# Windowed attention in four query groups of 144, its score and value products in eight array tiles, PSUM with fixed places

## The chip, the cores and the metric

One NeuronCore of a Trainium2 chip runs the whole program; the other cores are idle. The metric is the device time of one execution in microseconds. The engines are TensorE (PE, with its weight loads shown apart as PEld), VectorE (DVE), ScalarE (ACT), GpSimd (POOL) and SyncE (SP), which issues the DMAs. Each engine works through its own instructions in order.

## The reference

Eight batches of eight heads attend over 576 positions with a head dimension of 64. The first four heads see the last 32 positions, the last four see every fourth of the last 128, so that both kinds look at 32 keys. The result is a matrix of 4608 tokens by 512, which goes through a dense layer, a softmax gate with a normalisation, and a second dense layer.

```python
scores = scale * np.matmul(q, k.transpose(0, 1, 3, 2))
mask_plain = (rel >= 0) & (rel < window)                      # window = 32
mask_dil = (rel >= 0) & (rel < window * dilation) & (rel % dilation == 0)   # dilation = 4
attn = softmax(where(mask, scores, -1e9)); attn_out = attn @ v
x = attn_out.transpose(0, 2, 1, 3).reshape(B * S, H * D)      # 4608 x 512
h = x @ w_in                                                  # 512 -> 1024
solu = h * softmax(h)
ln = (solu - mean) / sqrt(var + 1e-06) * g_ln
out = ln @ w_out                                              # 1024 -> 512
```

## The kernel before

**Units.** A unit is one batch and one pair of heads; there are 32, numbered by batch and, inside a batch, by pair. Pairs 0 and 1 are plain heads, pairs 2 and 3 dilated ones, whose positions the host has sorted into four classes of 144, so that the same 32-wide window serves both. Queries go in blocks of 32, each against 64 keys (its own block and the one before).

**A unit's front** (`scores`, `soft_max`, `soft_exp`, `soft_inv`, `soft_norm`). `scores` multiplies in two parts, s0 and s1, into two PSUM tiles `ps_s0` and `ps_s1`. The 576 queries are split into two halves of nine blocks; the two heads lie on partitions 0 to 63 and 64 to 127 of `kt`, and the stationary operand `qt` has zeros where the other head is, so that one matmul over 128 rows and 64 columns gives both heads of a block (L163). VectorE adds the mask into `sm` (L171), takes the maximum (L187), GpSimd subtracts it (L188), ScalarE takes the exponential (L202), VectorE sums, inverts and multiplies (L204 to L214). For units 2, 3 and 4 the mask goes in by a matmul with an identity instead, and the exponential reads PSUM.

**A unit's back** (`probs_t`, `attend`, `spread`). VectorE transposes the probabilities in 32x32 blocks to `pt` (L221). `attend` multiplies them with `vt` in array tiles of 32 rows by 64 columns, four of the eight tiles in use, into `ps_x` and `ps_t1` (L235). `spread` copies the result, half by half, to the dense layer's operand: ScalarE writes the rounded part `x_hi` (L257) and VectorE the rest, `x_lo` (L258).

**A tile's dense part.** Each of 36 tiles of 128 tokens goes through `moe_h` (two halves of 12 matmuls into `ps_h`, L277), `moe_act` (VectorE's negated maximum `nmax` L288, ScalarE's exponential `e` L291), `moe_gate` (VectorE's product `t` L298, mean `mu` L306 and centring L307), `moe_var` (ScalarE and GpSimd), `moe_t` (eight transposes on TensorE into `ps_t0` and `ps_t1`, L336, copied out as `th` and `tl`) and `moe_o` (24 matmuls into `ps_o`, L351, of the tile before).

**Order.** The weights are converted and units 0 to 4 run in hand-written ticks, in which the order of all engines is that of the text. From the first tile on only TensorE's order is written (five lists `LEADS`, then `STEP` for every further tile); a scheduler orders the other engines. In `STEP`, on TensorE, a tile's dense layer h0 to h3 comes first, then x0 (`attend` of the unit whose front was in the step before), then s0 and s1 (`scores` of the next unit), then o (`moe_o`), then t (`moe_t`). 22 of the steps have both an x0 and the scores after it, four have x0 alone, three have scores alone, the last five neither.

**PSUM.** Eight pieces of one bank each, or two: `ps_s0`, `ps_s1`, `ps_x`, `ps_t0`, `ps_t1`, `ps_o` and `ps_h` (two). The scores share no piece with another step; `ps_t1` serves both `attend` and `moe_t`.

Of the kernel before, what the change touches and what calls it, by code (L numbers as in the profile page):

```python
# [68 lines left out]
def windowed_attention_then_solu_kernel(  # L69
# [70 lines left out]
    def scores(n, part):  # L140

        qt, kt = loaded[n]["q"], loaded[n]["k"]
        dil = int(n % NPAIR >= NPAIR // 2)
        if part == 0:
            st[n] = {"sm": att.tile([P, NU, WQ], F32, name="sm")}
        sm = st[n]["sm"]
        us = range(0, 5) if part == 0 else range(5, NU)
        nu = len(us)
# [1 line left out]
        ps = ps_a.tile([P, 512], F32, name=f"ps_s{part}")  # L150
        ps = ps[:, 0 : 5 * WQ].rearrange("p (u w) -> p u w", w=WQ)
        st[n]["ps", part] = ps
        mk = mask_sb[:, dil, us[0] : us[0] + nu, :]
# [6 lines left out]
        for i, u in enumerate(us):  # L160
            for par in range(2):
                qb = NU * par + u
                nc.tensor.matmul(  # L163
                    out=ps[64 * par : 64 * par + 64, i, :],
                    lhsT=qt[:, qb, :],
                    rhs=kt[:, WIN * qb : WIN * qb + WQ],
                    start=not on_pe,
                    stop=not on_pe or i == nu - 1,
                )
# [4 lines left out]

    def soft_max(n):
        sm = st[n]["sm"]
        mx = small.tile([P, NU], F32, name="mx")
        if n in PE_MASK:
            st[n]["mx"] = mx
            for part, (u0, u1) in enumerate(((0, 5), (5, 9))):  # L180
                nc.vector.tensor_reduce(
                    out=mx[:, u0:u1], in_=st[n]["ps", part][:, 0 : u1 - u0, :],
                    axis=AX.X, op=ALU.max, negate=True,
                )
# [2 lines left out]
        nc.vector.tensor_reduce(out=mx, in_=sm, axis=AX.X, op=ALU.max)  # L187
        nc.gpsimd.tensor_tensor(  # L188
            out=sm, in0=sm, in1=mx.unsqueeze(2).broadcast_to([P, NU, WQ]), op=ALU.subtract
        )  # L190

    def soft_exp(n):
        sm = st[n]["sm"]
        if n in PE_MASK:
            rs = st[n]["rs"] = small.tile([P, NU], F32, name="rs")
            for u in range(9):
                nc.scalar.activation(
                    out=sm[:, u, :], in_=st[n]["ps", u // 5][:, u % 5, :], func=AF.Exp,
                    bias=st[n]["mx"][:, u : u + 1], scale=0.125, accum_out=rs[:, u : u + 1],
                )  # L200
            return
        nc.scalar.activation(out=sm, in_=sm, func=AF.Exp, scale=0.125)  # L202
# [14 lines left out]

    def probs_t(n):

        pt = st[n]["pt"] = att.tile([P, NU * WQ], F32, name="pt")  # L220
        nc.vector.transpose(out=pt, in_=st[n]["sm"].rearrange("p u w -> p (u w)"))  # L221

    def attend(n):

        vt = loaded[n]["v"]
        pt = st[n]["pt"]
        b, pr = divmod(n, NPAIR)
        out = [ps_a.tile([P, 512], F32, name="ps_x"), ps_m.tile([P, 512], F32, name="ps_t1")]
        for i in range(NV):
            u0, u1 = max(i - 1, 0), min(i + 1, NU)  # L230
            k0, k1 = max(WQ * i - WIN, 0), min(WQ * i + WIN, NU * WQ)
            for par in range(2):
                for h in range(2):
# [1 line left out]
                    nc.tensor.matmul(  # L235
                        out=out[par][64 * h : 64 * h + 64, WIN * u0 : WIN * u1],
                        lhsT=vt[r : r + WIN, i, :],
                        rhs=pt[r : r + WIN, k0:k1],
                        start=i == 0,
                        stop=i == NV - 1,  # L240
                        skip_group_check=True,
                    )
        for half in range(2):
            spread(n, out[half][:, 0:HALF], half)

    def spread(n, ps, half):
        b, pr = divmod(n, NPAIR)
        base = (b % 2) * S

        def view(x):  # L250
            x = x[:, pr, base : base + S]
            if pr < NPAIR // 2:
                return x[:, half * HALF : half * HALF + HALF]
            return x.rearrange("p (i c) -> p c i", c=DIL)[:, 2 * half : 2 * half + 2, :]

        src = ps if pr < NPAIR // 2 else ps.rearrange("p (c i) -> p c i", c=2)
        nc.scalar.copy(out=view(x_hi), in_=src)  # L257
        nc.vector.tensor_tensor(  # L258
            out=view(x_lo), in0=src, in1=view(x_hi).bitcast(F32), op=ALU.subtract
        )  # L260
# [24 lines left out]
    def moe_act(i):  # L285
        h = ms[i]["h"].rearrange("p a b -> p (a b)")
        nmax = small.tile([P, 1], F32, name="nmax")
        nc.vector.tensor_reduce(out=nmax, in_=h, axis=AX.X, op=ALU.max, negate=True)  # L288
# [2 lines left out]
        nc.scalar.activation(out=e, in_=h, func=AF.Exp, bias=nmax, scale=1.0, accum_out=se)  # L291
# [256 lines left out]
def _mask():  # L548
    m = np.full((P, 2, NU, WQ), NEG, np.float32)
    c = np.arange(WQ)  # L550
    for u in range(NU):
        for p in range(P):
            qb = NU * (p // 64) + u
            q = WIN * qb + p % WIN
            k = WIN * (qb - 1) + c
            ok = (k >= 0) & (q - k >= 0) & (q - k < WIN)
            m[p, 0, u, ok] = 0.0
            m[p, 1, u, ok & (k // CLS == q // CLS)] = 0.0
    return m
# [47 lines left out]
```

## Time and profile before

| | |
|---|---|
| median of three runs | 577.02 us (576.15 to 577.3) |
| the profiled execution | 577.16 us, of which the span from the first to the last instruction is 575.1 us |
| TensorE's granted clock, mean | 0.967 |
| DMA, mean over the span | 102 GB/s |

How to read it: the profile gives one execution. Busy shares are of the span; the chain that ended last tells which work the end hung on, and a timeline gives the start and the length of single instructions in microseconds. Ends of matmuls are modelled, so the distance between the starts of two matmuls says more than their length. A matmul on float32 operands shows as two instructions.

### The profile page before, as it was taken

To read this page: it belongs to the slowest core of one execution; us is meant where nothing else is said; L and a number is where in the kernel's file an instruction comes from. 1 tells how busy PE (TensorE), PEld (TensorE's weight loads), DVE (VectorE), ACT (ScalarE), POOL (GpSimd) and SP (SyncE) were. 2 spreads that over 40 slices of the span, in tenths; PEclk is the share of its full clock that TensorE was granted. 3 is DMA by queue.
4 is the path that set the end of the run, shared out by engine and by line. 5 is a ranking of instruction groups with operands and counts; after the bars stand their busy time and mean duration, and the time that the engine had idled before them with its cause. 6 is when DMAs were issued, how large, how long until landed. Compare 5 with 4: busy or idle time off the path is not lost.

```text
span 575.1 us, 13371 instructions
## 1 busy us (share of the span) xinstructions
PE 531.8 (92%) x5740; PEld 442.2 (77%) x5740; DVE 356.7 (62%) x617; ACT 225.5 (39%) x451; POOL 153.9 (27%) x280
## 2 busy tenths in 40 slices
PE   3464859999999999999999999999999999999996
PEld 2353648888888888888888888888888888888885
DVE  4988995645666666655666666646666666634342
ACT  3467753343333333333333333333333333333232
POOL 2654771212222222211222222211222222211111
PEclk9966779999999999999999999999999999999999
DMA  8786620312333333323232333222333310001000
GB/s 316 233 305 248 200 73 34 106 61 88 103 106 104 105 104 99 103 58 98 96 110 95 106 105 106 98 83 81 114 105 103 96 49 19 19 19 38 18 19 36
DMA packets 22090, 58.40 MB, mean 102 GB/s; under 512 B 2704, under 2 KB 3088, under 8 KB 22032
## 3 DMA queue, kind: packets, MB, share of 16 engines
q1 hardware_dynamic: 22032, 57.55, 30.1%
q8 instruction: 45, 0.74, 0.5%
q14 instruction: 13, 0.11, 0.0%
HBM read 48.11 MB, written 9.44 MB: 100 GB/s over the span
## 4 chain that ended last, share of the span: by engine, by line
PE 83%; DVE 8%; ACT 3%; issue 2%; DMA 2%; POOL 1%; SPq 0%; ACTq 0%; DVEq 0%
PE ps_h L277 34%; PE ps_o L351 32%; PE ps_x L235 5%; PE ps_s L163 5%; PE ps_t L336 5%; DVE mag L399 1%; PE ps_t L235 1%; DVE nmax L288 1%; DVE mag L414 1%; DMA raw<-w_out 1%; DMA mask_sb<-mask 1%; ACT e L291 1%; POOL sm L188 1%; DVE rs L204 1%; DVE mag L407 1%
## 5 line engine op out<-in xcount | busy, mean ns | idle before, releaser
L277 PE MATMUL ps_h<-wi_hi,x_hi 128*128 128x512 f32 x288 | 117.6, 408 | 7.5 <-ACT x_hi L257 5.3
L351 PE MATMUL ps_o<-wo_hi,th 128*128 128x512 f32 x288 | 116.2, 404 | 0.8 <-ACT th L338 0.8
L277 PE MATMUL ps_h<-wi_hi,x_lo 128*128 128x512 f32 x288 | 114.2, 397 | 0.0
L277 PE MATMUL ps_h<-wi_lo,x_hi 128*128 128x512 f32 x288 | 113.7, 395 | 0.0
L351 PE MATMUL ps_o<-wo_hi,tl 128*128 128x512 f32 x288 | 113.1, 393 | 0.0
L351 PE MATMUL ps_o<-wo_lo,th 128*128 128x512 f32 x288 | 113.1, 393 | 0.0
L291 ACT ACTIVATE e<-ps_h,nmax 128x1024 f32<-128x1024 f32 x36 | 40.2, 1116 | 168.2 <-DVE nmax L288 168.2
L288 DVE TENSOR_REDUCE nmax<-ps_h 128x1 f32<-128x1024 f32 x36 | 44.0, 1223 | 81.2 <-PE ps_h L277 81.1
L298 DVE CUSTOM_DVE_ANT_0 t<-ps_h,e 128x1024 f32<-128x1024 f32 x36 | 44.1, 1224 | 41.9 <-ACT e L291 41.9
L277 PEld LDWEIGHTS ps_h<-wi_hi,x_hi 128*128 128x128 f32 x288 | 55.3, 192 | 18.5 <-ACT x_hi L257 6.0
L235 PEld LDWEIGHTS ps_x<-pt,vt 32*64 32x64 f32 x1280 | 44.1, 145 | 31.6 <-issue 19.8
L235 PE MATMUL ps_x<-pt,vt 32*64 32x64 f32 (+1 forms) x1280 | 47.7, 230 | 20.8 <-DVE pt L221 11.4
L314 POOL TENSOR_SCALAR se<-se 128x1 f32<-128x1 f32 x36 | 8.9, 246 | 214.9 <-ACT e L291 214.8
L202 ACT ACTIVATE sm<-sm 128x576 f32<-128x576 f32 x29 | 19.9, 685 | 117.5 <-POOL sm L188 117.5
L351 PEld LDWEIGHTS ps_o<-wo_hi,th 128*128 128x128 f32 x288 | 54.5, 189 | 13.4 <-ACT th L338 1.1
L277 PEld LDWEIGHTS ps_h<-wi_hi,x_lo 128*128 128x128 f32 x288 | 54.9, 190 | 12.7 <-DVE x_lo L258 1.0
L188 POOL TENSOR_TENSOR sm<-sm,mx 128x576 f32<-128x576 f32 x29 | 43.9, 1515 | 75.8 <-DVE mx L187 75.5
L351 PEld LDWEIGHTS ps_o<-wo_hi,tl 128*128 128x128 f32 x288 | 54.5, 189 | 12.0 <-DVE tl L339 0.4
L277 PEld LDWEIGHTS ps_h<-wi_lo,x_hi 128*128 128x128 f32 x288 | 55.3, 192 | 10.2
L351 PEld LDWEIGHTS ps_o<-wo_lo,th 128*128 128x128 f32 x288 | 54.5, 189 | 10.5
L339 DVE TENSOR_TENSOR tl<-ps_t,th 128x512 fp32r<-128x512 f32 x72 | 45.6, 672 | 25.5 <-ACT th L338 25.5
L163 PE MATMUL ps_s<-kt,qt 128*64 128x64 f32 x1152 | 45.9, 239 | 9.8 <-DMA qt<-qT 9.8
(60 smaller groups left out, 756.1 us busy)
## 6 DMA issues: line engine op xcount, KB each, us to landing
qt<-qT SPq DMA_DIRECT2D x32, 576.0 KB, 5.4
vt<-vw SPq DMA_DIRECT2D x32, 320.0 KB, 3.2
kt<-kT SPq DMA_DIRECT2D x32, 304.0 KB, 3.9
out<-ob SPq DMA_DIRECT2D x36, 256.0 KB, 2.0
raw<-w_in SPq DMA_DIRECT2D x8, 512.0 KB, 5.6
raw<-w_out SPq DMA_DIRECT2D x8, 512.0 KB, 4.3
mask_sb<-mask SPq DMA_DIRECT2D x2, 144.0 KB, 5.6
id_sb<-ident SPq DMA_DIRECT2D x1, 64.0 KB, 6.8
```

The lines of the kernel that those rows point to most:

```text
L163: nc.tensor.matmul(out=ps[64 * par : 64 * par + 64, i, :], lhsT=qt[:, qb, :], rhs=kt[:, WIN * qb : WIN * qb + WQ], start=not on_pe, stop=n ...
L188: nc.gpsimd.tensor_tensor(out=sm, in0=sm, in1=mx.unsqueeze(2).broadcast_to([P, NU, WQ]), op=ALU.subtract)
L202: nc.scalar.activation(out=sm, in_=sm, func=AF.Exp, scale=0.125)
L235: nc.tensor.matmul(out=out[par][64 * h : 64 * h + 64, WIN * u0 : WIN * u1], lhsT=vt[r : r + WIN, i, :], rhs=pt[r : r + WIN, k0:k1], start= ...
L277: nc.tensor.matmul(out=h[:, half, :], lhsT=a[:, kt, xs], rhs=w[:, kt, ws], start=(kt == 0 and k == 0), stop=(kt == KT - 1 and k == 2),)
L288: nc.vector.tensor_reduce(out=nmax, in_=h, axis=AX.X, op=ALU.max, negate=True)
L291: nc.scalar.activation(out=e, in_=h, func=AF.Exp, bias=nmax, scale=1.0, accum_out=se)
L298: nc.vector.tensor_tensor_reduce(out=t, in0=h, in1=ms[i]["e"], scale=1.0, scalar=0.0, op0=ALU.mult, op1=ALU.add, accum_out=mu,)
L314: nc.gpsimd.tensor_scalar(out=se, in0=se, scalar1=1e-9, scalar2=None, op0=ALU.add)
L336: nc.tensor.transpose(out=ps[:, f, :], in_=t[:, k * P : k * P + P], identity=id_sb)
L339: nc.vector.tensor_tensor(out=tl[:, fs], in0=ps, in1=th[:, fs].bitcast(F32), op=ALU.subtract)
L351: nc.tensor.matmul(out=o, lhsT=a[:, f, :], rhs=w[:, f, :], start=(f == 0 and k == 0), stop=(f == FT - 1 and k == 2),)
```

## The change

Every unit is cut into four query groups of 144 positions, one to each 32 partitions, in place of two halves of 288. A group has five blocks of 32 queries, the last half empty (16 of 32), so that a unit's probabilities hold 2 heads x 5 blocks x 64 keys = 640 columns, where they held 9 x 64 = 576. `qt` holds the queries densely, without the zeros. A score matmul uses 64 rows (one head) and 32 columns (one group), so that eight array tiles, two heads by four groups, are addressed one after the other. `attend` uses all eight tiles of 32 rows by 64 columns, and its four groups go to four banks. `spread` copies a whole unit at once.

PSUM becomes one tile `banks` with fixed places: 0 and 1 for `ps_h`, 2 for `ps_o`, 3 to 6 (columns 0 to 143 of each) for `ps_x`, 3 and 4 for the transposes, and for the scores banks 6 and 7, except units 0 to 4, which use 0 and 1. The orders `TICKS`, `LEADS` and `STEP` stay as they are; s0 now does the whole of `scores`, and the name s1 in them does nothing.

```diff
-NU = S // WIN // 2
-NV = NU + 1
-KPAD = WIN
+NG = P // WIN
+GQ = S // NG
+NS = -(-GQ // WIN)
+NV = NS + 1
+SPAN = GQ * (NG - 1) + WIN * NS
...
+    banks = psum.tile([P, 8, 512], F32, name="banks")
+    ps_h = banks[:, 0:2, :]
+    ps_o = banks[:, 2, :]
+    ps_x = banks[:, 3:7, 0:GQ]
+    ps_t = (banks[:, 3, :], banks[:, 4, :])
...
-        qt = units.tile([P, S // WIN, 2 * WIN], F32, name="qt", bufs=2)
-        kt = units.tile([P, KPAD + S], F32, name="kt", bufs=2)
+        qt = units.tile([P, SPAN], F32, name="qt", bufs=2)
+        kt = units.tile([P, WIN + SPAN], F32, name="kt", bufs=2)
...
-        vt = units.tile([P, NV, D], F32, name="vt", bufs=3)
+        vt = units.tile([P, NV, 2 * D], F32, name="vt", bufs=3)
...
-    def scores(n, part):
+    def scores(n):
...
+        at = 0 if n <= NPAIR else 6
+        ps = banks[:, at : at + 2, 0 : NS * WQ]
...
-        for i, u in enumerate(us):
-            for par in range(2):
-                qb = NU * par + u
-                nc.tensor.matmul(
-                    out=ps[64 * par : 64 * par + 64, i, :],
-                    lhsT=qt[:, qb, :],
-                    rhs=kt[:, WIN * qb : WIN * qb + WQ],
-                    start=not on_pe,
-                    stop=not on_pe or i == nu - 1,
-                )
+        for i in range(NS):
+            for h in range(2):
+                for c in range(NG):
+                    q0 = GQ * c + WIN * i
+                    nc.tensor.matmul(
+                        out=ps[WIN * c : WIN * c + WIN, h, WQ * i : WQ * i + WQ],
+                        lhsT=qt[D * h : D * h + D, q0 : q0 + WIN],
+                        rhs=kt[D * h : D * h + D, q0 : q0 + WQ],
+                        start=not on_pe,
+                        stop=True,
+                        skip_group_check=True,
+                    )
         if not on_pe:
             nc.vector.tensor_tensor(
-                out=sm[:, us[0] : us[0] + nu, :], in0=ps[:, 0:nu, :], in1=mk, op=ALU.add
+                out=sm.rearrange("p h s w -> p h (s w)"), in0=ps,
+                in1=mask_sb[:, dil, :].unsqueeze(1).broadcast_to([P, 2, NS * WQ]),
+                op=ALU.add,
             )
...
     def attend(n):
-        out = [ps_a.tile([P, 512], F32, name="ps_x"), ps_m.tile([P, 512], F32, name="ps_t1")]
-        for i in range(NV):
-            u0, u1 = max(i - 1, 0), min(i + 1, NU)
-            k0, k1 = max(WQ * i - WIN, 0), min(WQ * i + WIN, NU * WQ)
-            for par in range(2):
+        first = int(n % NPAIR >= NPAIR // 2)
+        for i in range(first, NV):
+            k0, k1 = max(WQ * i - WIN, 0), min(WQ * i + WIN, WQ * NS - WQ + WIN + GQ % WIN)
+            c0 = WIN * max(i - 1, 0)
+            if i == NS - 1:
+                k1 = min(k1, k0 + GQ - c0)
+            for c in range(NG):
                 for h in range(2):
-                    r = 64 * par + 32 * h
                     nc.tensor.matmul(
-                        out=out[par][64 * h : 64 * h + 64, WIN * u0 : WIN * u1],
-                        lhsT=vt[r : r + WIN, i, :],
-                        rhs=pt[r : r + WIN, k0:k1],
+                        out=ps_x[D * h : D * h + D, c, c0 : c0 + k1 - k0],
+                        lhsT=vt[WIN * c : WIN * c + WIN, i, D * h : D * h + D],
+                        rhs=pt[WIN * c : WIN * c + WIN, h, k0:k1],
...
-        for half in range(2):
-            spread(n, out[half][:, 0:HALF], half)
+        spread(n)
...
-        nc.scalar.copy(out=view(x_hi), in_=src)
+        nc.scalar.copy(out=view(x_hi), in_=ps_x)
         nc.vector.tensor_tensor(
-            out=view(x_lo), in0=src, in1=view(x_hi).bitcast(F32), op=ALU.subtract
+            out=view(x_lo), in0=ps_x, in1=view(x_hi).bitcast(F32), op=ALU.subtract
         )
...
-            "s0": lambda: scores(n, 0),
-            "s1": lambda: scores(n, 1),
+            "s0": lambda: scores(n),
```

The built program shows what this does to the order at the place where TensorE goes from x0 to the scores. These are TensorE's rows there in the step of the fifteenth tile (x0 of unit 16, scores of unit 17), the kernel before; a number behind a name is a buffer, and the brackets name the semaphores waited for, DMAHW those of DMAs and the others by engine.

```order
L235 MATMUL ps_x_2977<-pt_2957,vt_2635 64x64 x2
L235 MATMUL ps_t1_2978<-pt_2957,vt_2635 64x64 x2
L235 MATMUL ps_x_2977<-pt_2957,vt_2635 64x32 x2
L235 MATMUL ps_t1_2978<-pt_2957,vt_2635 64x32 x2
L163 MATMUL ps_s0_3024<-kt_2638,qt_2637 64x64 [waits DMAHW4_49,DMAHW3_49]
L163 MATMUL ps_s0_3024<-kt_2638,qt_2637 64x64 x9
L163 MATMUL ps_s1_3041<-kt_2638,qt_2637 64x64 x8
L351 MATMUL ps_o_3081<-wo_hi_88,th_2934 128x512 [waits Activation_49]
```

The scores wait there for their two DMAs alone. The same place of TensorE in the changed kernel, where L236 is `attend`, L164 `scores` and L347 `moe_o`:

```order
L236 MATMUL banks_89<-pt_3219,vt_2894 64x32 x5
L236 MATMUL banks_89<-pt_3219,vt_2894 64x64 x24
L236 MATMUL banks_89<-pt_3219,vt_2894 64x48 x8
L236 MATMUL banks_89<-pt_3219,vt_2894 64x16 x8
L164 MATMUL banks_89<-kt_2897,qt_2896 32x64 [waits DMAHW4_49,DMAHW3_49,DVE_49]
L164 MATMUL banks_89<-kt_2897,qt_2896 32x64 x39
L347 MATMUL banks_89<-wo_hi_85,th_3199 128x512 [waits Activation_49]
```

The first score matmul now also waits for VectorE. The value it waits for is the count that VectorE reaches with `x_lo` of the x0 just ahead, which reads bank 6. VectorE's rows in the same step, the kernel before:

```order
L288 TENSOR_REDUCE nmax_3036<-ps_h_2950 128x1 [waits PE_49]
L298 ISA t_3059,mu_3060<-ps_h_2950,e_3038 128x1024 [waits Activation_49]
L298 ISA mu_3060 128x1
L258 TENSOR_TENSOR x_lo_91<-ps_x_2977,x_hi_90 128x288 [waits Activation_49]
L258 TENSOR_TENSOR x_lo_91<-ps_t1_2978,x_hi_90 128x288 [waits Activation_49]
L171 TENSOR_TENSOR sm_3023<-ps_s0_3024,mask_sb_82 128x320 [waits PE_49]
L171 TENSOR_TENSOR sm_3023<-ps_s1_3041,mask_sb_82 128x256 [waits PE_49]
L306 TENSOR_SCALAR mu_3060<-mu_3060 128x1 [waits DVE_49]
L187 TENSOR_REDUCE mx_3051<-sm_3023 128x9 [waits DVE_49,Pool_49]
L307 TENSOR_SCALAR t_3059<-t_3059,mu_3060 128x1024 [waits DVE_49]
```

And in the changed kernel, where L286 is `nmax`, L296 the gate's product, L257 `x_lo`, L305 the centring, L173 the mask and L189 the maximum:

```order
L286 TENSOR_REDUCE nmax_3331<-banks_89 128x1 [waits PE_49]
L296 ISA t_3344,mu_3345<-banks_89,e_3333 128x1024 [waits Activation_49]
L296 ISA mu_3345 128x1
L257 TENSOR_TENSOR x_lo_88<-banks_89,x_hi_87 128x576 [waits Activation_49]
L304 TENSOR_SCALAR mu_3345<-mu_3345 128x1 [waits DVE_49]
L305 TENSOR_SCALAR t_3344<-t_3344,mu_3345 128x1024 [waits DVE_49]
L173 TENSOR_TENSOR sm_3289<-banks_89,mask_sb_79 128x640 [waits PE_49]
L189 TENSOR_REDUCE mx_3336<-sm_3289 128x10 [waits DVE_49,Pool_49]
```

`x_lo` stays behind the gate's product, in one instruction instead of two, and the mask and the maximum have moved behind the centring.

More of the change, by code (lines that the diff above doesn't have):

```diff
@@ L100, in windowed_attention_then_solu_kernel @@
     id_sb = const.tile([P, P], F32, name="id_sb")
-    mask_sb = const.tile([P, 2, NU, WQ], BF16, name="mask_sb")
+    mask_sb = const.tile([P, 2, NS * WQ], BF16, name="mask_sb")
     g_sb = const.tile([P, FT], F32, name="g_sb")
@@ L138, in windowed_attention_then_solu_kernel @@
     st = {}
-    def scores(n, part):
+    def scores(n):
         qt, kt = loaded[n]["q"], loaded[n]["k"]
         dil = int(n % NPAIR >= NPAIR // 2)
[L144 to L148, printed above, removed]
+        at = 0 if n <= NPAIR else 6
+        ps = banks[:, at : at + 2, 0 : NS * WQ]
+        st[n] = {"ps": ps.rearrange("p h (s w) -> p h s w", w=WQ)}
+        sm = st[n]["sm"] = att.tile([P, 2, NS, WQ], F32, name="sm")
@@ L149, in scores @@
         on_pe = n in PE_MASK
[L150 to L153, printed above, removed]
         if on_pe:
-            for c in range(0, P, 64):
+            for h in range(2):
                 nc.tensor.matmul(
-                    out=ps[c : c + 64, 0:nu, :], lhsT=id_bf[:, c : c + 64], rhs=mk,
-                    start=True, stop=False,
-                )
@@ new lines, in scores @@
+        for i in range(NS):
+            for h in range(2):
+                for c in range(NG):
[8 more added lines that the diff above has]
+                    )
@@ L178, in soft_max @@
         if n in PE_MASK:
[L179 to L184, printed above, removed]
+            nc.vector.tensor_reduce(out=mx, in_=st[n]["ps"], axis=AX.X, op=ALU.max, negate=True)
             nc.gpsimd.tensor_scalar(out=mx, in0=mx, scalar1=0.125, scalar2=None, op0=ALU.mult)
@@ L187, in soft_max @@
         nc.vector.tensor_reduce(out=mx, in_=sm, axis=AX.X, op=ALU.max)
-        nc.gpsimd.tensor_tensor(
-            out=sm, in0=sm, in1=mx.unsqueeze(2).broadcast_to([P, NU, WQ]), op=ALU.subtract
-        )
+        nc.gpsimd.tensor_tensor(out=sm, in0=sm, in1=wide(mx), op=ALU.subtract)
     def soft_exp(n):
         sm = st[n]["sm"]
+        rs = st[n]["rs"] = small.tile([P, 2, NS], F32, name="rs")
         if n in PE_MASK:
[L195 to L200, printed above, removed]
+            for h in range(2):
+                for i in range(NS):
+                    nc.scalar.activation(
+                        out=sm[:, h, i, :], in_=st[n]["ps"][:, h, i, :], func=AF.Exp,
+                        bias=st[n]["mx"][:, h, i : i + 1], scale=0.125,
+                        accum_out=rs[:, h, i : i + 1],
+                    )
             return
         nc.scalar.activation(out=sm, in_=sm, func=AF.Exp, scale=0.125)
-        rs = st[n]["rs"] = small.tile([P, NU], F32, name="rs")
         nc.vector.tensor_reduce(out=rs, in_=sm, axis=AX.X, op=ALU.add)
@@ L213, in soft_norm, with probs_t @@
         eng = nc.gpsimd if n < NPAIR + POOL_NORM else nc.vector
-        eng.tensor_tensor(
-            out=sm, in0=sm, in1=rs.unsqueeze(2).broadcast_to([P, NU, WQ]), op=ALU.mult
-        )
-    def probs_t(n):
-        pt = st[n]["pt"] = att.tile([P, NU * WQ], F32, name="pt")
-        nc.vector.transpose(out=pt, in_=st[n]["sm"].rearrange("p u w -> p (u w)"))
+        eng.tensor_tensor(out=sm, in0=sm, in1=wide(rs), op=ALU.mult)
+    def probs_t(n):
+        pt = st[n]["pt"] = att.tile([P, 2, NS * WQ], F32, name="pt")
+        nc.vector.transpose(
+            out=pt.rearrange("p h w -> p (h w)"), in_=st[n]["sm"].rearrange("p h s w -> p (h s w)")
+        )
     def attend(n):
@@ L242, in attend, with spread @@
                     )
-        for half in range(2):
-            spread(n, out[half][:, 0:HALF], half)
-    def spread(n, ps, half):
+        spread(n)
+    def spread(n):
         b, pr = divmod(n, NPAIR)
@@ L252, in view @@
             if pr < NPAIR // 2:
[L253 to L257, printed above, removed]
+                return x.rearrange("p (c i) -> p c i", c=NG)
+            return x.rearrange("p (i c) -> p c i", c=NG)
+        nc.scalar.copy(out=view(x_hi), in_=ps_x)
         nc.vector.tensor_tensor(
-            out=view(x_lo), in0=src, in1=view(x_hi).bitcast(F32), op=ALU.subtract
+            out=view(x_lo), in0=ps_x, in1=view(x_hi).bitcast(F32), op=ALU.subtract
         )
-        if half == 1:
-            del st[n], loaded[n]
+        del st[n], loaded[n]
     ms = {}
@@ L268, in moe_h @@
         if half == 0 and kts[0] == 0:
-            ms[i] = {"h": ps_m.tile([P, 2, 512], F32, name="ps_h")}
-        h = ms[i]["h"]
+            ms[i] = {}
+        h = ps_h
         assert reached[-1] >= KT * (half + 1)
@@ L285, in moe_act @@
     def moe_act(i):
-        h = ms[i]["h"].rearrange("p a b -> p (a b)")
+        h = ps_h.rearrange("p a b -> p (a b)")
         nmax = small.tile([P, 1], F32, name="nmax")
@@ L294, in moe_gate @@
     def moe_gate(i):
-        h = ms[i]["h"].rearrange("p a b -> p (a b)")
+        h = ps_h.rearrange("p a b -> p (a b)")
         t = moe.tile([P, DF], F32, name="t", bufs=T_BUFS)
@@ L332, in moe_t @@
         for c in range(2):
-            ps = ps_m.tile([P, 512], F32, name=f"ps_t{c}").rearrange("p (f q) -> p f q", q=P)
+            ps = ps_t[c].rearrange("p (f q) -> p f q", q=P)
             for f in range(4):
@@ L344, in moe_o @@
     def moe_o(i, fs):
-        if fs[0] == 0:
-            ms[i]["o"] = ps_m.tile([P, DO], F32, name="ps_o")
         assert reached[-1] == len(cv)
-        o, th, tl = ms[i]["o"], ms[i]["th"], ms[i]["tl"]
+        o, th, tl = ps_o, ms[i]["th"], ms[i]["tl"]
         for f in fs:
@@ L548, in _mask @@
 def _mask():
-    m = np.full((P, 2, NU, WQ), NEG, np.float32)
+    m = np.full((P, 2, NS, WQ), NEG, np.float32)
     c = np.arange(WQ)
-    for u in range(NU):
+    for s in range(NS):
         for p in range(P):
[L553 to L559, printed above, removed]
+            q0 = GQ * (p // WIN) + WIN * s
+            q = q0 + p % WIN
+            k = q0 - WIN + c
+            ok = (q >= S) | ((k >= 0) & (q - k >= 0) & (q - k < WIN))
+            m[p, 0, s, ok] = 0.0
+            m[p, 1, s, ok & ((q >= S) | (k // CLS == q // CLS))] = 0.0
+    return m.reshape(P, 2, NS * WQ)
 def _bits(a):
```

34 lines of the change are left out of this document (16 added, 18 removed).

## The prediction

> **What bounds the kernel now.** I read the page first: its span, the busy shares and the chain that ended last.
>
> ```profile
> span 575.1 us, 13371 instructions
> PE 531.8 (92%) x5740; PEld 442.2 (77%) x5740; DVE 356.7 (62%) x617; ACT 225.5 (39%) x451; POOL 153.9 (27%) x280
> PE 83%; DVE 8%; ACT 3%; issue 2%; DMA 2%; POOL 1%; SPq 0%; ACTq 0%; DVEq 0%
> ```
>
> TensorE is busy 92% of the span and 83% of the chain. After the start tile follows tile on it; the busy times by window show one whole step there, from the last dense matmul of one tile to that of the next.
>
> ```profile
> 267.60:282.09 14.49, 14.49 (x173) 12.15 (x172) 9.25 (x17) 5.06 (x10) 3.68 (x7) 1.00 0.31 104
> ```
>
> The second number is TensorE: busy for all 14.49 us, with the clock at 1.00, VectorE for 9.25. So a microsecond taken off TensorE's path here is a microsecond off the time, and one in which it stands still is lost. TensorE's timeline of that step:
>
> ```profile
> 267.60 0.39 PE L277 MATMUL ps_h<-wi_hi,x_lo 128*128 128x512 f32 x1
> 267.92 0.24 PE L235 MATMUL ps_x<-pt,vt 32*64 32x32 f32 x2
> ...
> 268.14 0.22 PE L235 MATMUL ps_x<-pt,vt 32*64 32x64 f32 x2
> 268.15 0.22 PE L235 MATMUL ps_t<-pt,vt 32*64 32x64 f32 x2
> 268.20 0.22 PE L235 MATMUL ps_x<-pt,vt 32*64 32x64 f32 x2
> 268.21 0.22 PE L235 MATMUL ps_t<-pt,vt 32*64 32x64 f32 x2
> ...
> 269.21 1.27 PE L163 MATMUL ps_s<-kt,qt 128*64 128x64 f32 x36
> 270.41 0.50 PE L351 MATMUL ps_o<-wo_hi,th 128*128 128x512 f32 x1
> ```
>
> x0 takes 269.21 - 267.92 = 1.29 us for 80 instructions, the scores 270.41 - 269.21 = 1.20 us for 36. Four value instructions, one to an array tile, start within about 0.02 us, and the next four 0.058 us after them (268.14, 268.20). So a round costs 0.058 us however many tiles take part, as long as their starts fit in: x0 is 20 rounds of four, the scores 18 rounds of two (18 x 0.058 = 1.05, and 0.15 for the change of array shape).
>
> **The change, part by part.** *Scores.* 80 instructions over eight tiles are 10 rounds: 1.20 - 8 x 0.058 = 0.73 us, a gain of 0.47. Eight starts at the spacing of four in 0.02 us need under 0.058, so I take the whole gain; the other end is no gain at all, if tiles that share rows of the array take turns. *Values.* Plain units have 12 rounds, dilated 10, against 20: about 0.7 us, a gain of 0.6, the other end again none.
>
> *The new wait.* `x0` now fills banks 3 to 6 and the scores behind it need 6 and 7. They may start once `x_lo` has read bank 6, and the order rows above keep `x_lo` behind `nmax` and the gate's product on VectorE. What that chain takes stands in the timeline of before, VectorE and ScalarE, first a step whose x0 is of a plain unit, then one of a dilated unit.
>
> ```profile
> 268.02 1.22 DVE L288 TENSOR_REDUCE nmax<-ps_h 128x1 f32<-128x1024 f32 x1 [3.13 <-PE ps_h L277]
> 270.58 1.23 DVE L298 CUSTOM_DVE_ANT_0 t<-ps_h,e 128x1024 f32<-128x1024 f32 x1 [1.33 <-ACT e L291]
> 271.73 0.45 DVE L258 TENSOR_TENSOR x_lo<-ps_x,x_hi 128x288 fp32r<-128x288 f32 x1
> 272.10 0.45 DVE L258 TENSOR_TENSOR x_lo<-ps_t,x_hi 128x288 fp32r<-128x288 f32 x1
> ```
> ```profile
> 269.34 1.12 ACT L291 ACTIVATE e<-ps_h,nmax 128x1024 f32<-128x1024 f32 x1 [5.28 <-DVE nmax L288]
> 270.73 0.41 ACT L257 CAST x_hi<-ps_t 128x288 fp32r<-128x288 f32 x1
> ```
> ```profile
> 297.01 1.23 DVE L288 TENSOR_REDUCE nmax<-ps_h 128x1 f32<-128x1024 f32 x1 [1.97 <-PE ps_h L277]
> 300.72 0.66 DVE L258 TENSOR_TENSOR x_lo<-ps_x,x_hi 128x288 fp32r<-128x288 f32 x1
> 301.29 0.65 DVE L258 TENSOR_TENSOR x_lo<-ps_t,x_hi 128x288 fp32r<-128x288 f32 x1
> ```
>
> `nmax` waits for the last dense matmul, ScalarE's `e` for `nmax`, the product for `e`, and `x_lo` stands behind it: it starts 3.71 us after `nmax` does, in both (271.73 - 268.02, 300.72 - 297.01). Nothing the change shortens lies on this chain; `x_hi` is done by 271.14, before it matters. One `x_lo` of 576 columns in place of two of 288 (together 0.82 and 1.22 us) I put at 0.78 and 1.20, a little under the pair. From VectorE's end to TensorE's start I take the 0.14 us of another such wait, the centring and the transposes of the step with scores alone:
>
> ```profile
> 260.53 0.75 DVE L307 TENSOR_SCALAR t<-t,mu 128x1024 f32<-128x1024 f32 x1
> 261.42 0.41 PE L336 MATMUL ps_t<-id_sb,t 128*128 128x128 f32 x2
> ```
>
> So the scores start 3.71 + 0.78 + 0.14 = 4.63 us after `nmax` in a plain step and 5.05 in a dilated one; now they start 269.21 - 268.02 = 1.19 us after it. They come 3.44 and 3.86 us later. Of the 22 steps with both, 12 have an x0 of a plain unit and 10 of a dilated one: 12 x 3.44 + 10 x 3.86 = **+79.9 us**. The faster x0 is no gain there, since the wait swallows it. Behind the waiting matmul stand moe_o and moe_t, which need nothing of it: TensorE keeps its order, so they wait too. The shorter scores do count: 22 x 0.47 = **-10.3 us**.
>
> *What is late next.* Behind the scores come mask, maximum, subtraction, exponential, sum, scaling and transposition, all on 640 columns now, and the next x0 needs them.
>
> ```profile
> L188 POOL TENSOR_TENSOR sm<-sm,mx 128x576 f32<-128x576 f32 x29 | 43.9, 1515 | 75.8 <-DVE mx L187 75.5
> L202 ACT ACTIVATE sm<-sm 128x576 f32<-128x576 f32 x29 | 19.9, 685 | 117.5 <-POOL sm L188 117.5
> L221 DVE STREAM_TRANSPOSE pt<-sm 128x576 f32<-128x576 f32 x32 | 24.8, 776 | 0.9
> ```
>
> Five VectorE operations of about 0.78, the subtraction of 1.5 and the exponential of 0.7 make 6.1 us, with a tenth on top 6.7; two more for waits between the engines would make 9. TensorE has moe_o, moe_t and a whole dense layer to do meanwhile, 282.09 - 270.41 = 11.7 us. I cost it at nothing.
>
> *Steps without the wait.* Four steps with x0 alone gain 0.6 each, three with scores alone about 0.5 (there the centring above nearly ends the wait of the transposes): **-3.9 us**.
>
> *The clock.* TensorE stands still from the end of x0 (about 0.7 us after `nmax`) to the scores: 3.9 us in a plain step, 4.3 in a dilated one. The start of the kernel shows what pauses do. These are windows between changes of the granted clock, 3.41 us each; the first number pair is TensorE's busy time, the clock stands behind POOL.
>
> ```profile
> 60.94:64.36 3.42, 3.24 (x119) 2.62 (x117) 3.33 (x5) 2.87 (x5) 3.15 (x3) 1.00 0.79 249
> 64.36:67.77 3.41, 1.35 (x6) 1.05 (x6) 3.41 (x9) 3.40 (x7) 1.22 (x3) 1.00 0.89 311
> 67.77:71.18 3.41, 3.41 (x14) 2.81 (x13) 3.41 (x5) 2.43 (x5) 3.10 (x3) 0.50 0.72 240
> ...
> 74.60:78.01 3.41, 1.32 (x37) 1.13 (x36) 3.41 (x5) 1.61 (x3) 3.41 (x3) 1.00 0.32 80
> 78.01:81.42 3.41, 0.00 (x0) 0.00 (x0) 3.41 (x5) 1.34 (x2) 1.46 (x2) 0.50 0.47 185
> 81.42:84.84 3.42, 2.60 (x81) 2.54 (x82) 3.36 (x6) 1.93 (x3) 1.78 (x2) 0.50 0.02 5
> 84.84:88.25 3.41, 3.41 (x9) 2.64 (x9) 2.87 (x6) 1.58 (x5) 2.56 (x5) 0.50 0.32 96
> ```
>
> A window with 1.3 us of work is followed by one at half the clock, one with 3.24 is not; and from half the clock a window with 2.60 did not lead back to full. A pause of 4.1 us leaves at least one window with under 1.5 us of work wherever it falls. If between 1.9 and 3.4 us of it lie in its first window (44% of the positions), the second is at half, with about 1.95 us of work in it, and by the row with 2.60 the third too: (1.95 + 3.41) / 2 = 2.7 us lost. In the other positions one window is at half: 1.5 to 1.7 us. The mean is 2.1, times 22 **+46 us**. The ends are 0 (no half clock at all) and 2.7 in every step, 59.
>
> *The start.* Its DMAs and VectorE change both: `qt` shrinks from 1152 to 592 columns, and VectorE's softmax work grows from 576 to 640.
>
> ```profile
> PE ps_s L163 <- DMA qt<-qT: 9.8, 2, 5.4
> ```
>
> TensorE waits 9.8 us for queries there, of which a halved transfer could give back up to 5; seven units with five VectorE operations that are 64 columns longer (776 / 576 x 64 = 0.09 us each by L221) cost about 3. I take 0, with 5 us to either side.
>
> The sum against the profiled execution: 575.1 + 79.9 - 10.3 - 3.9 + 46 = 687 us of span, and 577.16 - 575.1 = 2.1 around it: **689 us**. Its own time stands 0.14 us over the median of the runs shown.
>
> **The rivals.** *The clock holds.* Of the rows above, those with a pause are from the start, where the work is mixed; if a pause must fill a window to bring the clock down, only (4.1 - 3.41) / 3.41 = 20% of the pauses do, each at 1.7 us: 22 x 0.2 x 1.7 = 7 in place of 46, and the time is 650 us. Against it: the two windows with 1.35 and 1.32 us of work were not empty, and half the clock followed. The Trainium skill, on "TensorE: Matmul & The Clock Gate", section "What's actually happening", speaks for this rival: it has the clock fall after at least one idle window of about 3.4 us. Taken by the letter the two rows disagree with it.
>
> *The tiles take turns.* If eight tiles run no faster than the rounds of before, the 10.3 and the 3.9 us are not gained: 703 us. For it: the trace shows no two tiles that share rows other than in the scores. Against it: those two do share all rows, and run side by side.
>
> *The wait isn't there, and it gets faster.* It decides at one point: the scores break even if they start at most 1.19 + 0.47 = 1.66 us after `nmax`, that is if `x_lo` ends by 1.5 us. Then all 22 steps gain 0.47 + 0.6: 577.2 - 22 x 1.07 - 3.9 = 550 us. Against it: the order rows put `x_lo` behind the product, and the product waits for `e` there (idle 1.33 us in its row). A scheduler's other order would have to show in those rows.
>
> **How the numbers follow.** Both the wait and the half clock as costed: 0.70, which is the forecast, 689 us. The clock holds: 0.17. The tiles take turns: 0.10. Faster: 0.02, no change 0.01. Changes under 0.2% can't be told from none here. The likeliest case alone reaches from 675 to 703 (the clock's mean at 1.7 to 2.5 us a pause, 9 us to either side, and the start's 5). The range must take in half of the first rival and part of the second: 648 to 712.
>
> **What would show it.** Right: TensorE's weight loads of L164 wait for VectorE's `x_lo` L257, 22 times, 3.7 to 4.5 us each, some 90 us in all; a granted clock near 0.8 with halves after each wait; VectorE's `x_lo` still 3.7 us behind `nmax`; score instructions in groups of eight per 0.058 us; no wait of x0 for `pt`. A mean clock above 0.93 would show the first rival, scores of 1.2 us at full clock the second. What would make it wrong altogether is an `x_lo` ahead of the gate's product, or a further wait behind the late scores that I costed at nothing.

## The result, and the profile after

The changed kernel takes 690.16 us (median of 4 runs, 688.75 to 690.84) against 576.97 us (576.15 to 577.3) before: a ratio of 1.196 [1.194, 1.199]. The forecast was 689 us. The profiled execution took 689.79 us, with a span of 688.0 us against 575.1: 112.9 us more. The page of the changed kernel, the lines that answer to those of before (the third is the granted clock in 40 slices, the fourth the chain that ended last):

```profile
span 688.0 us, 16592 instructions
PE 555.5 (81%) x7398; PEld 453.4 (66%) x7398; DVE 370.9 (54%) x553; ACT 230.2 (33%) x425; POOL 139.8 (20%) x280
PEclk9998788998888899999888889999888889999999
PE 72%; DVE 18%; ACT 6%; issue 2%; DMA 1%; SPq 0%; POOL 0%; ACTq 0%; DVEq 0%
```

TensorE was busy 92% of the span and is now busy 81%. VectorE's share of the chain went from 8 to 18%, ScalarE's from 3 to 6%: what used to run beside TensorE now stands between two pieces of its work. The list of waits says where (in all, times, the longest):

```profile
PEld banks L164 <- DVE mu L304: 82.7, 22, 4.0
PE banks L164 <- DVE mu L304: 80.6, 22, 4.0
```

22 times the scores' weight loads and matmuls (L164) stand still, up to 4.0 us each. The list names `mu`; the timeline shows that this name is off by one. A step whose x0 is of a dilated unit, on VectorE, ScalarE and TensorE:

```profile
263.71 1.23 DVE L286 TENSOR_REDUCE nmax<-banks 128x1 f32<-128x1024 f32 x1 [3.84 <-PE banks L275]
266.27 1.22 DVE L296 CUSTOM_DVE_ANT_0 t<-banks,e 128x1024 f32<-128x1024 f32 x1 [1.33 <-ACT e L289]
267.42 1.16 DVE L257 TENSOR_TENSOR x_lo<-banks,x_hi 128x576 fp32r<-128x576 f32 x1
268.48 0.15 DVE L304 TENSOR_SCALAR mu<-mu 128x1 f32<-128x1 f32 x1
```
```profile
265.03 1.11 ACT L289 ACTIVATE e<-banks,nmax 128x1024 f32<-128x1024 f32 x1 [6.00 <-DVE nmax L286]
```
```profile
263.60 1.08 PE L236 MATMUL banks<-pt,vt 32*64 32x64 f32 x80
268.63 1.04 PE L164 MATMUL banks<-kt,qt 64*32 64x64 f32 x80 [3.95 <-DVE mu L304]
269.60 0.79 PE L347 MATMUL banks<-wo_hi,th 128*128 128x512 f32 x1
```

`x_lo` ends at 267.42 + 1.16 = 268.58 and the scores start at 268.63. `mu` only touches a column of its own, and the scores have no use for it; it is the next instruction on VectorE, and it started just ahead of the moment at which TensorE was let go. The scores themselves go from 268.63 to 269.60 (the start of moe_o): 0.97 us. The clock, in windows of 3.41 us over the same step, and the step as a whole from the last dense matmul of one tile to that of the next:

```profile
262.73:266.15 3.42, 1.95 (x85) 1.42 (x83) 1.23 (x1) 1.12 (x3) 0.00 (x0) 1.00 0.17 24
266.15:269.56 3.41, 0.93 (x80) 0.88 (x80) 3.12 (x5) 1.21 (x3) 0.65 (x3) 1.00 0.27 96
269.56:272.98 3.42, 3.42 (x18) 2.71 (x9) 1.64 (x2) 1.10 (x2) 2.07 (x4) 0.50 0.55 182
272.98:276.39 3.41, 3.41 (x16) 2.80 (x16) 2.34 (x5) 0.74 (x1) 0.12 (x1) 1.00 0.00 0
263.28:282.88 19.60, 15.65 (x218) 12.80 (x216) 10.16 (x15) 5.82 (x9) 2.84 (x7) 0.91 0.21 67
```

After the window with 1.95 us of TensorE work the clock stays whole; after the one with 0.93 us it is at half for a window. The last row is the step: 19.60 us, where before one took 14.49. Its parts add up: the scores start 268.63 - 263.71 = 4.92 us after `nmax` and not 1.19, +3.73; they are 0.23 shorter; the half window costs 1.71. 14.49 + 3.73 - 0.23 + 1.71 = 19.70.

Summed over the trace in the same way: the wait +77.2 us (12 plain steps with 4.51, 10 dilated with 4.92, against 1.19), shorter scores -5.1, the seven steps with x0 or scores alone -2.7, the start +0.2. What is left of the 112.9 us, 43, is the half clock. The step shown is one of nine with one half window, which costs them 1.4 us on average; the other thirteen have two, of which the first begins in the pause, at a cost of 2.4.

### The profile page after: what moved, and what is told of

Read it like the earlier page. It is cut to its first block, busy times and chain, and to the rows that moved or that the text cites. A ratio compares the mean times of both kernels' runs of the same rounds, so it can differ in the third digit from the quotient of the medians.

```text
span 688.0 us, 16592 instructions
## 1 busy us (share of the span) xinstructions
PE 555.5 (81%) x7398; PEld 453.4 (66%) x7398; DVE 370.9 (54%) x553; ACT 230.2 (33%) x425; POOL 139.8 (20%) x280
## 4 chain that ended last, share of the span: by engine, by line
PE 72%; DVE 18%; ACT 6%; issue 2%; DMA 1%; SPq 0%; POOL 0%; ACTq 0%; DVEq 0%
PE banks L347 34%; PE banks L275 27%; PE banks L164 5%; DVE nmax L286 4%; PE banks L334 4%; DVE t L296 4%; ACT e L289 4%; DVE x_lo L257 3%; DVE mag L395 1%; ACT sm L198 1%; DVE mag L410 1%; DVE mag L403 1%; PE banks L236 1%; DMA mask_sb<-mask 1%; DVE mag L424 1%
## 5 line engine op out<-in xcount | busy, mean ns | idle before, releaser
L347 PE MATMUL banks<-wo_hi,th 128*128 128x512 f32 x288 | 133.5, 463 | 0.8 <-ACT th L336 0.8
L347 PE MATMUL banks<-wo_lo,th 128*128 128x512 f32 x288 | 126.8, 440 | 0.0
L347 PE MATMUL banks<-wo_hi,tl 128*128 128x512 f32 x288 | 125.4, 436 | 0.0
L275 PE MATMUL banks<-wi_hi,x_hi 128*128 128x512 f32 x288 | 117.0, 406 | 1.6 <-ACT sm L198 1.6
L164 PE MATMUL banks<-kt,qt 64*32 64x64 f32 x2560 | 42.1, 287 | 92.4 <-DVE mu L304 80.6
L275 PE MATMUL banks<-wi_lo,x_hi 128*128 128x512 f32 x288 | 113.7, 395 | 0.0
L275 PE MATMUL banks<-wi_hi,x_lo 128*128 128x512 f32 x288 | 113.5, 394 | 0.0
L286 DVE TENSOR_REDUCE nmax<-banks 128x1 f32<-128x1024 f32 x36 | 44.0, 1223 | 123.1 <-PE banks L275 123.1
L164 PEld LDWEIGHTS banks<-kt,qt 64*32 64x32 f32 x2560 | 34.8, 135 | 99.7 <-DVE mu L304 82.7
L347 PEld LDWEIGHTS banks<-wo_hi,th 128*128 128x128 f32 x288 | 64.0, 222 | 18.6 <-issue 3.2
L347 PEld LDWEIGHTS banks<-wo_hi,tl 128*128 128x128 f32 x288 | 63.0, 219 | 15.6 <-DVE tl L337 0.4
L347 PEld LDWEIGHTS banks<-wo_lo,th 128*128 128x128 f32 x288 | 64.4, 224 | 13.3
L296 DVE CUSTOM_DVE_ANT_0 t<-banks,e 128x1024 f32<-128x1024 f32 x36 | 44.1, 1224 | 44.3 <-ACT e L289 44.3
L236 PE MATMUL banks<-pt,vt 32*64 32x64 f32 (+3 forms) x2816 | 39.6, 242 | 31.7 <-DVE pt L220 26.1
L236 PEld LDWEIGHTS banks<-pt,vt 32*64 32x64 f32 x2816 | 36.2, 144 | 42.3 <-DVE pt L220 27.2
L275 PEld LDWEIGHTS banks<-wi_lo,x_hi 128*128 128x128 f32 x288 | 55.1, 191 | 10.2
L311 ACT ACTIVATE e<-t 128x1024 f32<-128x1024 f32 x36 | 38.1, 1057 | 68.6 <-DVE t L305 68.6
```

The lines of the kernel that those rows point to most:

```text
L164: nc.tensor.matmul(out=ps[WIN * c : WIN * c + WIN, h, WQ * i : WQ * i + WQ], lhsT=qt[D * h : D * h + D, q0 : q0 + WIN], rhs=kt[D * h : D * ...
L236: nc.tensor.matmul(out=ps_x[D * h : D * h + D, c, c0 : c0 + k1 - k0], lhsT=vt[WIN * c : WIN * c + WIN, i, D * h : D * h + D], rhs=pt[WIN * ...
L275: nc.tensor.matmul(out=h[:, half, :], lhsT=a[:, kt, xs], rhs=w[:, kt, ws], start=(kt == 0 and k == 0), stop=(kt == KT - 1 and k == 2),)
L296: nc.vector.tensor_tensor_reduce(out=t, in0=h, in1=ms[i]["e"], scale=1.0, scalar=0.0, op0=ALU.mult, op1=ALU.add, accum_out=mu,)
L311: nc.scalar.activation(out=e, in_=t, func=AF.Square, accum_out=sq)
L347: nc.tensor.matmul(out=o, lhsT=a[:, f, :], rhs=w[:, f, :], start=(f == 0 and k == 0), stop=(f == FT - 1 and k == 2),)
```

## The experiments

**Is it the wait, or the new shapes?** Theory A: the scores wait for `x_lo`, because scores and x0 have bank 6 in common, and the clock falls in that pause. Theory B: the narrower tiles or the longer softmax are slow in themselves. The first run takes the wait away by issuing the scores ahead of the dense layer:

```diff
-    "h0 t0 h1 t1 h2 t2 h3 x0 x1 s0 act s1 max exp inv gate var lv lq norm o t"
+    "s0 h0 t0 h1 t1 h2 t2 h3 x0 x1 act s1 max exp inv gate var lv lq norm o t"
```

> The changed kernel with the scores moved to the front of each step, ahead of the dense layer (h0), in STEP and in the one list of LEADS that has x0 and then the scores. Banks 6 and 7 have long been read there. Theory A (the time went into the wait of the scores for x_lo and into the half clock that follows it): both vanish, the scores cost 0.97 us and x0 about 1.1 where they cost 1.20 and 1.29, some 0.4 us a unit less than before: 565 us (558 to 580, the upper end if VectorE is late with the maximum of the dense layer), mean clock 0.96. Theory B (the new shapes, the larger number of instructions or the shared banks themselves are slow): it stays above 650.

Measured: 606.48 us (604.98 to 607.72), ratio to before 1.052 [1.050, 1.055]. The wait for `x_lo` is gone, and 84 us with it, which B does not allow. After the start only 2 us are at half clock. But 41 us are missing to the expected time, and the list of waits shows another one in its place:

```profile
PEld banks L334 <- DVE t L305: 41.3, 25, 2.3
DVE tl L337 <- ACT th L336: 78.2, 33, 3.5
```

Now the transposes (L334) wait for the centring (L305), in 25 steps. The mask's and the maximum's turn on VectorE comes earlier, and the scheduler, which orders VectorE and ScalarE here, put them ahead of `nmax` and behind `tl`, which waits for ScalarE's `th`:

```profile
274.63 1.29 DVE L337 TENSOR_TENSOR tl<-banks,th 128x512 fp32r<-128x512 f32 x2 [2.33 <-ACT th L336]
275.83 0.82 DVE L173 TENSOR_TENSOR sm<-banks,mask_sb 128x640 f32<-128x640 f32 x1
276.75 0.82 DVE L189 TENSOR_REDUCE mx<-sm 128x10 f32<-128x640 f32 x1
...
281.77 1.22 DVE L286 TENSOR_REDUCE nmax<-banks 128x1 f32<-128x1024 f32 x1
```

The third tile's line, written out apart, moves the scores as well, to a place between two parts of the dense layer. Only TensorE's order was moved by hand; the orders of the other engines stayed with the scheduler and came out differently.

The second run leaves the wait and takes away what it does to the clock. Matmuls without use fill the pause:

```diff
+    def fill():
+        for _ in range(34):
+            nc.tensor.matmul(
+                out=banks[:, 7, 320:512], lhsT=wi_hi[:, 0, 0:P], rhs=wi_hi[:, 0, 0:192],
+                start=True, stop=True, skip_group_check=True,
+            )
...
+        if front is not None and mid is not None and i >= 2:
+            ops["x0"] = lambda: (attend(mid), fill())
```

> The changed kernel, with 34 matmuls of 128x192 that nobody reads (into the free columns of bank 7) issued between x0 and the scores, in the steps that have both. They take about 3.2 us and fill most of the pause, and the order and the wait stay. Theory A: the scores still start 4.5 and 4.9 us after nmax, but the clock stays full: 690 - 43 = 647 us (640 to 656), mean clock 0.96. If the half clock costs little and something else is late behind the scores, it stays at 675 or more.

Measured: 653.61 us (652.79 to 654.52), granted clock 0.989 against 0.903. TensorE and `x_lo` in a plain step:

```profile
315.72 4.04 PE L248 MATMUL banks<-wi_hi 128*128 128x192 f32 x34
319.69 1.04 PE L164 MATMUL banks<-kt,qt 64*32 64x64 f32 x80
```
```profile
314.70 1.23 DVE L293 TENSOR_REDUCE nmax<-banks 128x1 f32<-128x1024 f32 x1 [3.87 <-PE banks L282]
318.41 0.75 DVE L264 TENSOR_TENSOR x_lo<-banks,x_hi 128x576 fp32r<-128x576 f32 x1
```

`x_lo` ends at 319.16, and the fill holds the scores until 319.69, 4.98 us after `nmax` where a plain step of the changed kernel has 4.51. So the fill is 0.47 us too long in 12 steps and 0.06 in ten, 6.2 us; without that it would be 647, as expected. TensorE does more work and the kernel is 690.2 - 653.6 = 36.6 us faster, 43 with the excess taken off: that is the price of the clock, shown by itself.

The third run is the kernel before with the wait alone. The scores' first part takes the buffer of x0's output:

```diff
-        ps = ps_a.tile([P, 512], F32, name=f"ps_s{part}")
+        ps = ps_a.tile([P, 512], F32, name="ps_x" if part == 0 and n > NPAIR else f"ps_s{part}")
```

> The kernel before with one edit: the first part of the scores of units 5 on takes the PSUM buffer of ps_x instead of its own, so that it waits for the first half of x_lo. Shapes, instructions and everything else are those of before. Theory A: the scores start 3.71 + 0.45 (plain) or 0.66 (dilated) + 0.05 us after nmax instead of 1.19, 22 x 3.1 = 68 us, and TensorE pauses for about 3.1 us each time, which brings half the clock for another 25 to 43: 577 + 68 + 34 = 679 us (665 to 690). Theory B: 577 to 585.

Measured: 697.79 us (695.09 to 700.95), ratio 1.210 [1.205, 1.215]. The old shapes with the wait are slower than the whole change, so B falls as the cause of the loss. The wait in the list, and TensorE in a step of it:

```profile
PEld ps_x L163 <- DVE x_lo L258: 69.5, 22, 3.3
```
```profile
318.20 1.33 PE L163 MATMUL ps_x<-kt,qt 128*64 128x64 f32 x20 [2.95 <-DVE x_lo L258]
319.32 1.07 PE L163 MATMUL ps_s<-kt,qt 128*64 128x64 f32 x16
320.32 0.80 PE L351 MATMUL ps_o<-wo_hi,th 128*128 128x512 f32 x1
```

Here the list names `x_lo` itself. The scores start 4.21 us (plain) and 4.42 us (dilated) after `nmax`, 68.6 us in all, as expected. The rest, 697.8 - 576.8 - 68.6 = 52 us (576.8 is the median of before taken beside these runs), is dearer than expected. One reason is that at half clock the old scores take 320.32 - 318.20 = 2.12 us where the new ones take 104.82 - 103.49 = 1.33, here in the changed kernel:

```profile
103.49 1.40 PE L164 MATMUL banks<-kt,qt 64*32 64x64 f32 x80 [3.95 <-DVE mu L304]
104.82 0.79 PE L347 MATMUL banks<-wo_hi,th 128*128 128x512 f32 x1
```

The fourth puts the scores ahead of x0, which then needs the mask to have read bank 6 (in the third tile's line too):

```diff
-    "h0 t0 h1 t1 h2 t2 h3 x0 x1 s0 act s1 max exp inv gate var lv lq norm o t"
+    "h0 t0 h1 t1 h2 t2 h3 s0 x0 x1 act s1 max exp inv gate var lv lq norm o t"
```

> The changed kernel with the scores directly ahead of x0, behind the dense layer. Then x0 waits for bank 6 until VectorE has added the mask, which needs no exponential: about 1.3 + 0.85 us after nmax. Theory A: a pause of about 1 us in each of 22 steps, too short for the clock: o starts about 3.2 us after nmax where it did 2.4 before, 577 + 18 = 595 us (586 to 606), mean clock above 0.95. If pauses of 1 us bring half the clock as well, 615 to 640. Theory B: above 650.

Measured: 594.98 us (594.27 to 597.49), ratio 1.032 [1.030, 1.035]. The wait turned round, and it is short, since the mask depends on nothing but the scores:

```profile
321.64 1.04 PE L164 MATMUL banks<-kt,qt 64*32 64x64 f32 x80
322.60 0.36 PE L236 MATMUL banks<-pt,vt 32*64 32x64 f32 x12
323.76 0.91 PE L236 MATMUL banks<-pt,vt 32*64 32x64 f32 x68 [0.80 <-DVE sm L173]
```

Twelve instructions of x0 that go to the other banks run, and the 13th waits 0.80 us. Pauses of about 1 us cost next to no clock: after the start only 6 us are at half.

**Would other columns of the same bank do?** x0 needs 144 columns of bank 6, the scores 320; there is room for both.

```diff
-        ps = banks[:, at : at + 2, 0 : NS * WQ]
+        ps = banks[:, at : at + 2, 512 - NS * WQ : 512]
```

> The changed kernel with the scores in columns 192 to 512 of banks 6 and 7 in place of 0 to 320; x0 uses columns 0 to 144 of bank 6, so the two share a bank and no column. If the scores wait by bank, as the program's order of waits says: 690 us (686 to 694), scores still 4.5 and 4.9 us after nmax. If by column: the wait is gone, 565 us (560 to 575).

Measured: 687.32 us in one run, and the wait stands as it stood:

```profile
PEld banks L164 <- DVE mu L304: 82.7, 22, 4.0
```

The dependence that this kernel's program carries goes by the bank and not by the columns. With 2 banks for `ps_h`, 1 for `ps_o`, 4 for x0 and 2 for the scores, nine are wanted and there are eight.

**A version that is faster than both.** From the third tile on, all four engines go by an order written out by hand. The scores stand between two parts of the dense layer, so the mask and the maximum are over before `nmax`, and the row sum falls into VectorE's wait for `e` (`act` is split into `nmax` and `e`, `gate` into `prod` and `centre`, and `spread`, the copy of x0's output into `x_hi` and `x_lo`, has a place of its own):

```diff
-    "p t h0 h1 t0 h2 t1 h3 t2 x0 s0 act s1 x1 max p exp inv lv norm gate lq t var",
-    "h0 t0 h1 t1 h2 h3 s0 t2 x0 x1 act s1 gate p max exp inv lv t norm var lq",
-    "t0 h0 h1 t1 h2 t2 x0 h3 x1 act s0 s1 max exp inv lv p gate norm t lq var",
+    "p t t0 h0 h1 s0 max h2 h3 x0 nmax exp inv e prod spread centre norm var pt p lv lq t",
...
-    "h0 t0 h1 t1 h2 t2 h3 x0 x1 s0 act s1 max exp inv gate var lv lq norm o t"
+    "t0 h0 h1 s0 max h2 h3 x0 nmax exp inv e prod spread centre norm var pt lv lq o t"
...
+        if i == len(LEADS) - 1:
+            hand.close()
+            ctx.enter_context(
+                tc.manual_schedule(engines={ET.PE, ET.DVE, ET.Activation, ET.Pool})
+            )
```

> The changed kernel with its shapes and banks, but from the third tile on all engines go by an order written out by hand: scores between the second and third part of the dense layer, the mask and the maximum ahead of nmax, then on VectorE nmax, the row sum, its inverse, the product, x_lo, the centring, the scaling, the transposition; on ScalarE the softmax's exponential ahead of e. So the scores' wait for x_lo should be gone and x0 should wait for nothing. Theory A (the shapes are a small gain, the loss is the wait and the clock that falls in it): x0 1.30 to about 0.95 and the scores 1.20 to about 1.0 in 22 steps, 22 x 0.55 = 12, the other steps 2.5, one more change of array shape a step back, 22 x 0.1 = 2: 564 us (558 to 572). Theory B (the new shapes are slow themselves, or the late softmax holds something up): 577 or more.

The same order with the shapes of the kernel before, so that order and shapes can be told apart:

> The kernel before, with its shapes, in the same hand-written order of all engines. Tells what of the hand-ordered changed kernel is the order and what the shapes. If the order is worth nothing: 577 plus one more change of array shape in 22 steps at 0.1 us, 579 us (575 to 584), and the shapes are then worth 15 us. If the order is the gain: 566 or less.

Measured: 569.39 us (568.97 to 569.8) with the new shapes, ratio to before 0.988 [0.985, 0.990], a gain of 1.2% that is small but clear of the noise, and 578.43 us (577.41 to 580.76) with the old ones, ratio 1.003 [1.001, 1.004]. The order alone costs 1.6 us; the new shapes in it are worth 9.0 us. TensorE of the hand-ordered new shapes, one step by windows, then the instructions on it, and VectorE:

```profile
279.17:293.51 14.34, 14.34 (x233) 11.66 (x232) 9.56 (x15) 5.27 (x9) 2.84 (x8) 1.00 0.27 80
```
```profile
279.49 1.20 PE L234 MATMUL banks<-pt,vt 32*64 32x32 f32 x96
...
289.92 1.04 PE L162 MATMUL banks<-kt,qt 64*32 64x64 f32 x80
290.89 0.50 PE L272 MATMUL banks<-wi_hi,x_hi 128*128 128x512 f32 x1
```
```profile
277.54 0.82 DVE L187 TENSOR_REDUCE mx<-sm 128x10 f32<-128x640 f32 x1
279.60 1.23 DVE L287 TENSOR_REDUCE nmax<-banks 128x1 f32<-128x1024 f32 x1 [1.24 <-PE banks L272]
280.74 0.81 DVE L203 TENSOR_REDUCE rs<-sm 128x10 f32<-128x640 f32 x1
...
282.15 1.22 DVE L305 CUSTOM_DVE_ANT_0 t<-banks,e 128x1024 f32<-128x1024 f32 x1
...
283.31 0.75 DVE L254 TENSOR_TENSOR x_lo<-banks,x_hi 128x576 fp32r<-128x576 f32 x1
```

TensorE is busy 14.34 of 14.34 us at full clock. `x_lo` ends at 284.06, and the next scores come at 289.92: nearly 6 us lie between the two that touched in the changed kernel. The expected 564 was 5 us too low for two reasons. The dense layer cut in two by the scores takes 0.24 us more (5.87 us for both parts, 5.63 whole), where I had put 0.1; and x0 takes 1.01 us (dilated) or 1.13 us (plain), where I had put 0.95. The shapes' own part adds up: 24 x 0.23 (scores) + 14 x 0.29 + 12 x 0.17 (x0) = 11.6 us, less a steady part that starts 2.7 us later, 8.9 us against the measured 9.0.

**What paces the scores?** They took 0.97 us and not 0.73. In the trace the first 32 instructions come as predicted, eight per 0.056 us, and the rest more slowly. Each group of eight is issued twice, in units 5 to 31:

```diff
-            for h in range(2):
+            for h in [0, 1] * (1 if on_pe or n <= NPAIR else 2):
```

> The hand-ordered changed kernel in which every score group of eight is issued twice in the 25 units of the steady part (the second writes the same values again). The prediction's rule, 0.058 us a round of eight however many tiles take part: ten rounds more, +0.58 us a unit, +14.5 us, 579 us. If the supply of instructions sets the pace, 16.6 ns a pair of weight load and matmul: +80 x 16.6 ns = 1.33 us a unit, +33 us, 597 us.

Measured: 592.58 us (591.03 to 593.77), 23.2 us over the hand-ordered kernel; neither expectation. TensorE:

```profile
286.38 1.80 PE L162 MATMUL banks<-kt,qt 64*32 64x64 f32 x160
288.11 0.50 PE L272 MATMUL banks<-wi_hi,x_hi 128*128 128x512 f32 x1
```

160 instructions take 288.11 - 286.38 = 1.73 us, 0.76 more than 80, in 24 of the 25 units of the steady part (25 x 0.76 = 19 us; the remaining unit of the profiled run stalls for 2 us, and a window at half clock follows). That is 9.5 ns an instruction, 0.076 us a round of eight. Rounds at 0.058 hold for four rounds only, and 16.6 ns is the pace at half clock, which I had taken for a limit that does not depend on the clock. x0 of the changed kernel, which has other shapes, slows at the same place: in the x0 of a dilated unit at 283.20 the first 32 instructions take 0.29 us and the next 32 take 0.37. Whether the later pace is set by the array or by what feeds it stays open.

## Why the prediction was right, point by point

*The wait* was sized at 79.9 us and measured 77.2. Each link held: `x_lo` starts 267.42 - 263.71 = 3.71 us after `nmax`, to the hundredth; one `x_lo` of 576 columns takes 0.75 and 1.16 us (put at 0.78 and 1.20); only from VectorE's end to TensorE's start it is 0.05 us and not the 0.14 taken from another wait.

*The shorter scores* were the mis-sized term: 22 x 0.47 = 10.3 us predicted, 22 x 0.23 = 5.1 measured at full clock. The step that failed is "so I take the whole gain": the spacing of 0.058 us was read off rounds of four tiles and carried over to ten rounds of eight. *The values* failed at the same place: x0 gains 0.29 us (dilated) and 0.17 us (plain), not 0.6. It cost little, since x0's gain vanishes in the wait anyway. *The steps without the wait*: 3.9 us predicted, 2.7 measured.

*The clock* was put at 46 us, and is 43, by difference and by the filled pause. The mechanism held, and its two parts erred against each other: two half windows were put in 44% of the positions at 2.7 us, and came in 13 of the 22 steps (59%) at 2.4; the other steps were put at 1.5 to 1.7 us and lost 1.4. The rival "the clock holds" falls. On this the Trainium skill, "TensorE: Matmul & The Clock Gate", section "What's actually happening", says that the clock falls after at least one idle window of about 3.4 us; the window above from 266.15 was not idle, it had 0.93 us of work in it, and half the clock followed. The trace does not agree with the page, and the measurement decides. "A granted clock near 0.8" was a slip: 46 us lost are 92 us at half, which with before's 0.967 makes a mean of about 0.90, and 0.903 was granted.

*The start* came out at +0.2 us against the 0 of the sum. *What is late next* came to nothing, as costed: x0 waits for no `pt` in the steady part. The rival "the tiles take turns" was half true: four rounds go side by side, the rest some 40% slower (32 instructions in 0.33 us are 0.082 us a round). The errors partly cancelled: -2.7 (wait), -3 (clock), +5.2 (scores), +1.2 (other steps), and the span came out 1 us over the predicted 687. That the forecast came within about 1 us is partly luck; that the kernel got some 110 us slower, by the wait and by the clock behind it, is not.

## What to carry to other kernels

Where a buffer gets a fixed place, ask for each bank who reads it last and when, and what on the bottleneck's queue now stands behind that reader; here one shared bank outweighed the gain of better shapes by more than ten times. A pause on TensorE must be priced twice, once for its length and once for the clock behind it: 3.5 us of waiting cost 2 us more at half speed, while pauses of about 1 us, and the transposes' waits of up to 2.3 us in the first experiment, cost next to nothing more. Where one engine's order is moved, the orders of the engines that feed it have to move with it, or a new wait takes the old one's place.
